# Attention scores from two fp32r parts in the two row halves of the array, with two heads in one exponential

## The chip, the cores and the metric

The kernel runs on one core of one Trainium2 chip. Its time is the device time of the whole kernel in microseconds; three runs of the kernel before took 4031.95, 4031.96 and 4034.76 us, so the median is 4031.96 us. A profile is one further execution, recorded instruction by instruction.

The engines are named as the profile names them: PE multiplies matrices (PEld is its loading of the stationary operand, the "weights"), DVE, ACT and POOL are the vector, activation and general engines, and SP issues most DMAs. PE writes only to PSUM, which has eight banks; one bank holds 512 fp32 numbers in each of 128 partitions.

## The reference

Two layers run one after the other, each an attention block and then an MLP, on an input of 2048 rows by 512 columns in fp32. Each block adds its result to its input.

```python
B, S, D, H = 1, 2048, 512, 32          # so a head has Dh = 16 columns
# attention, on the layer-normed x
qkv = (x @ wqkv).reshape(B, S, 3, H, Dh)
scores = einsum("bhqd,bhkd->bhqk", q, k) * (Dh ** -0.5)
p = softmax(scores)                     # over k
o = einsum("bhqk,bhkd->bhqd", p, v)     # then @ wo
# MLP, F = 1792, on the layer-normed x
h = x @ w1 + b1
act = h * tanh(softplus(h));  return act @ w2
```

The softmax takes the maximum over the 2048 keys from each score, so the kernel needs every score twice in effect: once for the maximum and once for the exponential.

## The kernel before, in words

**Precision.** The dense products (`mm3`, lines 111 to 116) split each fp32 operand into a high and a low fp32r part and add three products. The scores are made otherwise: q and k are split into three bf16 parts each (lines 380 to 389) and the parts are stacked along the contraction. `K_PARTS` and `Q_PARTS` name the six pairs of parts; six pairs of 16 columns give `KROWS` = 96 contraction rows. Two more rows carry the negative maximum of each query (as two bf16 parts, against rows of ones), so that the score matmul of 98 rows (`MROWS`) gives the score less its maximum.

**Groups and steps.** The 32 heads are done in 8 groups of 4 (`HG`). A group has 4 blocks of 512 queries and 16 key tiles of 128 keys, so 64 steps; a layer has 512 steps and the kernel 1024. `prep_qk` (line 186) loads the stacked q and k of a group from a DRAM scratch, half a group ahead; `prep_v` (line 208) lays out the values.

**One step** (`run`, lines 327 to 350) does three things:

- `score` (line 273), once for each of the 4 heads: a matmul of 128 keys by 512 queries into one PSUM bank (line 280, tile `sc`), then the exponential on ACT from this bank into the tile `p` (line 287). The banks come from `pbank("s", ...)`, a pool of three separate one-bank tiles.
- `max_mm` (line 219), four times, for a step 20 steps (`AHEAD`) later: 128 queries by 512 keys (line 236, tile `pm`), two of them into a two-bank tile `mx`, of which there are two; DVE then reduces the 1024 columns to one maximum per query (line 245). After 16 steps `max_fold` and `max_rows` bring the maxima into rows of q by a transpose on PE, two DVE instructions and eight small DMAs.
- `pv` (line 289) for the step before: exponentials times values, four heads in four column groups of the array, in plain fp32 (line 299). The program has 4 such matmuls per step and the profile shows 8, two for each. After 16 steps `out_rows` transposes and divides by the sum.

**The order on PE** is written out by hand. `pe` (line 175) chains every attention matmul to the one before, so PE does them in the order of the calls: score 0, score 1, max 0, 1, 2, score 2, max 3, score 3, `pv` of the step before. What `tick` brings in (`max_rows`, `out_rows`) stands before `pv`. ACT and DVE serve their queues in order too; outside the attention a scheduler orders the instructions.

**Other users of the three "s" banks.** The accumulators `qk` of the q and k projection (line 378, read by an ACT copy and a DVE subtraction), `va` of the values (line 401, read by an ACT copy), the hidden layer `h` of the MLP (line 448, read by an ACT instruction at line 468), and some transposes (`nmt`, `otp`, `op`).

Of the kernel before, what the change touches and what calls it, by code (L numbers as in the profile page):

```python
# [9 lines left out]
F32 = mybir.dt.float32  # L10
F32R = mybir.dt.float32r
BF16 = mybir.dt.bfloat16
AF = mybir.ActivationFunctionType
ALU = mybir.AluOpType
# [4 lines left out]
P = 128  # L19
# [10 lines left out]
SCALE = DH ** -0.5  # L30
HCLAMP = 10.0
LN_HALF = -0.6931471805599453
KROWS = 96
MROWS = 98
K_PARTS = (0, 0, 0, 1, 1, 2)
Q_PARTS = (0, 1, 2, 0, 1, 0)
AHEAD = 20
GSTEPS = NCH * NKT
STEPS = NG * GSTEPS
# [7 lines left out]
def kernel(ctx: ExitStack, tc: tile.TileContext, x, wqkv, wo, w1, b1, w2, out):  # L47
# [14 lines left out]
    nc.gpsimd.memset(mhalf, -0.5)  # L62
    lnhalf = const.tile([P, 1], F32, name="lnhalf")
    nc.gpsimd.memset(lnhalf, LN_HALF)
    ones = const.tile([MROWS - KROWS, 256], BF16, name="ones")
    nc.gpsimd.memset(ones, 1.0)
    b1t = const.tile([P, FT], F32, name="b1t")
    nc.sync.dma_start(b1t, b1.rearrange("(f p) -> p f", p=P))
# [1 line left out]
    def b8(shape, dt, name):  # L70
        return blk.tile(shape, dt, tag="blk", name=name)

    def pbank(tag, name):
        return ps.tile([P, 512], F32, tag=tag, name=name, bufs=3 if tag == "s" else 1)

    def t512(tag, name, dt=F32):
        return tmp.tile([P, 512], dt, tag=tag, name=name, bufs=T_BUFS.get(tag, 2))
# [29 lines left out]
    def split_psum(hi, lo, src):  # L107
        nc.scalar.activation(hi, src, AF.Copy)
        nc.vector.tensor_tensor(lo, src, hi.bitcast(F32), op=ALU.subtract)
# [52 lines left out]
    class Attention:  # L162
# [24 lines left out]
        def prep_qk(self, g):  # L187
            l = self.l
            ks, qs = [], []
            for u in range(HG // 2):  # L190
                k = b8([P, 2, S], BF16, f"ks{l}{g}{u}")
                q = b8([P, 2, S], BF16, f"qs{l}{g}{u}")
                nc.sync.dma_start(
                    k[KROWS:MROWS].rearrange("p h (r n) -> p (h r) n", n=256),
                    ones[:, None, :].to_broadcast([MROWS - KROWS, 2 * S // 256, 256]),
                )
                m, h0 = divmod(g * HG + 2 * u, P // DH)
                for t, parts, base in ((k, K_PARTS, NCH), (q, Q_PARTS, 0)):
                    for j, a in enumerate(parts):
                        nc.sync.dma_start(  # L200
                            t[j * DH : (j + 1) * DH],
                            self.scr[base + m][a, h0 * DH : (h0 + 2) * DH, :].rearrange("(h d) n -> d h n", d=DH),
                        )
                ks.append(k)
                qs.append(q)
            self.qk[g] = (ks, qs)
# [9 lines left out]
                )  # L216
            self.va[g] = va

        def max_mm(self, s, n):
            if s >= STEPS:  # L220
                return
            b, i = divmod(s, NKT)
            g, qb = divmod(b, NCH)
            h, qt = divmod(i, NCH)
            half, j = divmod(n, 2)
            l = self.l
            if n == 0 and s % GSTEPS == GSTEPS // 2 and g + 1 < NG:
                self.prep_qk(g + 1)
            ks, qs = self.qk[g]
            if i == 0 and n == 0:  # L230
                self.mxs[b] = tmp.tile([P, HG, NCH, 2], F32, tag="mxv", name=f"mxv{l}{b}")
            if j == 0:
                self.pm = ps.tile([P, 2, 512], F32, tag="mx", name=f"pm{l}{b}{i}{half}")
            q0 = qb * CW + qt * P
            self.pe(
                nc.tensor.matmul(  # L236
                    self.pm[:, j],
                    qs[h // 2][0:KROWS, h % 2, q0 : q0 + P],
                    ks[h // 2][0:KROWS, h % 2, ts(n, 512)],
                    start=True,  # L240
                    stop=True,
                )
            )
            if j == 1:
                nc.vector.tensor_reduce(self.mxs[b][:, h, qt, half : half + 1], self.pm, axis=AX.XY, op=ALU.max)  # L245
                if i == NKT - 1 and half == 1:
                    self.max_fold(b)

        def max_fold(self, b):
            l = self.l  # L250
# [6 lines left out]
        def max_rows(self, b, nm):  # L257
            g, qb = divmod(b, NCH)
            l = self.l
            _, qs = self.qk[g]  # L260
            tp = pbank("s" if self.running else "acc", f"nmt{l}{b}")
            self.pe(nc.tensor.transpose(tp[0 : HG * NCH, 0:P], nm, ident))
            np_ = tmp.tile([HG * NCH, 2, P], BF16, tag="np", name=f"np{l}{b}")
            nc.vector.tensor_copy(np_[:, 0], tp[0 : HG * NCH, 0:P])
            nc.vector.tensor_tensor(np_[:, 1], tp[0 : HG * NCH, 0:P], np_[:, 0], op=ALU.subtract)
            for h in range(HG):
                for a in range(2):
                    nc.sync.dma_start(
                        qs[h // 2][KROWS + a : KROWS + a + 1, h % 2, ts(qb, CW)].rearrange("o (t n) -> o t n", n=P),
                        np_[h * NCH : (h + 1) * NCH, a, :],  # L270
                    )

        def score(self, s, h):
            b, kt = divmod(s, NKT)
            g, qb = divmod(b, NCH)
            ks, qs = self.qk[g]
            if h == 0:
                self.pts[s] = b8([P, HG, CW], F32, f"p{self.l}{s}")
            sp = pbank("s", f"sc{self.l}{s}{h}")
            self.pe(nc.tensor.matmul(  # L280
                sp,
                ks[h // 2][0:MROWS, h % 2, ts(kt, P)],
                qs[h // 2][0:MROWS, h % 2, ts(qb, CW)],
                start=True,
                stop=True,
            ))
            nc.scalar.activation(self.pts[s][:, h, :], sp, AF.Exp, scale=SCALE)  # L287

        def pv(self, s):
            b, kt = divmod(s, NKT)  # L290
# [18 lines left out]
        def out_rows(self, b, ot):  # L309
            g, qb = divmod(b, NCH)  # L310
            l = self.l
            tp = pbank("s", f"otp{l}{b}")
            for t in range(NCH):
                self.pe(nc.tensor.transpose(tp[:, ts(t, P)], ot[:, ts(t, P)], ident))
            tv = tp.rearrange("p (t h d) -> p t h d", t=NCH, h=HG)
            rc = tmp.tile([P, NCH, HG, 1], F32, tag="rc", name=f"rc{l}{b}")
            nc.vector.reciprocal(rc, tv[:, :, :, DH : DH + 1])
            nc.vector.tensor_tensor(
                self.ost[qb][:, :, ts(g, HG * DH)].rearrange("p t (h d) -> p t h d", d=DH),
                tv[:, :, :, 0:DH],  # L320
                rc.to_broadcast([P, NCH, HG, DH]),
                op=ALU.mult,
            )

        def run(self, hooks, ost, fill):
            ost.extend(b8([P, NCH, D], F32, f"o{self.l}{c}") for c in range(NCH))
            self.ost = ost
            self.prep_v(0)
            self.running = True
            for s in range(STEPS):  # L330
                if s % GSTEPS == GSTEPS - NKT and s // GSTEPS + 1 < NG:
                    self.prep_v(s // GSTEPS + 1)
                self.score(s, 0)
                self.score(s, 1)
                for n in range(3):
                    self.max_mm(s + AHEAD, n)
                self.score(s, 2)
                self.max_mm(s + AHEAD, 3)
                if s + AHEAD >= STEPS:
                    next(fill, None)  # L340
                self.score(s, 3)
                self.tick()
                if s:
                    self.pv(s - 1)
                if s in hooks:
                    hooks[s]()
            self.pv(STEPS - 1)
            self.tick(99)
# [6 lines left out]
                wts[j] = load_rows(wqkv[:, 2 * D : 3 * D], j - 4, f"wv{l}{j}", **kw)  # L355

    def qkv(l, wts, tt, order, late):
        scr = [dram.tile([3, P, S], BF16, name=f"scr{l}{m}") for m in range(2 * NCH)]
        att = Attention(l, scr)
        ahead = [0]  # L360

        def some_max():
            if ahead[0] < AHEAD:
                att.chained = True
                att.tick()
                for n in range(4):
                    att.max_mm(ahead[0], n)
                ahead[0] += 1

        done = 0  # L370
        for m, c in order:
            if c not in tt:
                late()
            w = wts[m // 2]
            pt = tmp.tile([P, 3, CW], BF16, tag="raw", name=f"pt{l}{m}{c}", bufs=3)
            th, tl = tt[c]
            acc = pbank("s", f"qk{l}{c}{m}")
            mm3(
# [1 line left out]
                [(w[:, 0, k, ts(m % 2, P)], w[:, 1, k, ts(m % 2, P)], th[:, k], tl[:, k]) for k in range(KT)],  # L380
                pe=att.pe,
            )
            p0, p1, p2 = (pt[:, a] for a in range(3))
            r = t512("f", f"pr{l}{c}{m}")
            nc.scalar.activation(p0, acc, AF.Copy)
            nc.vector.tensor_tensor(r, acc, p0, op=ALU.subtract)  # L386
            nc.scalar.activation(p1, r, AF.Copy)
            nc.gpsimd.tensor_tensor(p2, r, p1, op=ALU.subtract)
            nc.scalar.dma_start(scr[m][:, :, ts(c, CW)].rearrange("a p n -> p a n"), pt)
            if (m, c) == (5, 3) and 4 not in wts:  # L390
                load_qkv(l, wts, (4, 5), behind=True)
            if m in (0, 4):
# [235 lines left out]
```

## Time and profile before

| what | value |
|---|---|
| median of three runs | 4031.96 us |
| span of the profiled execution | 4036.3 us (0.1% above the median; no other time of this execution is recorded) |
| PE busy | 3985.8 us, 99% of the span |
| DVE, ACT, POOL busy | 76%, 67%, 14% |
| first and last score matmul of the kernel | 195.4 us, 3668.9 us |
| granted PE clock, mean | 0.996 of full speed |

An instruction's time in the profile runs from its start to its modelled end. Matmuls overlap, so the distance from one start to the next is what a matmul costs PE in a stream, and its own duration is what a reader of its result waits for. In a grouped row ("x3") the duration is the union over the group. `<-` names what an engine waited for.

### The profile page before, as it was taken

Reading aid. Unit: us, or ns where it says so; the run is one execution under the profiler, and the core shown is the slowest. Engines: PE = TensorE matmul, PEld = TensorE weight load, DVE = VectorE, ACT = ScalarE, POOL = GpSimd, SP = SyncE. Lnnn points to the kernel's source line nnn. Section 1 sums busy time; section 2 is a strip of 40 time slices with the busy share of each in tenths; the row PEclk is TensorE's granted clock in tenths of the full one; section 3 lists DMA queues with packets and bytes.
Section 4 is the critical chain, followed back from the end, with each engine's and each line's share of the span. In section 5 each row is a group of like instructions: output and inputs, shape, how many; then the busy total and the mean of one; then the engine's idle time right before and its main releaser. Section 6 shows DMA issues by size and latency. Waiting matters only on the chain.

```text
span 4036.3 us, 54209 instructions
## 1 busy us (share of the span) xinstructions
PE 3985.8 (99%) x21312; PEld 1753.5 (43%) x21312; DVE 3075.2 (76%) x3266; ACT 2697.6 (67%) x4875; POOL 568.7 (14%) x465
## 2 busy tenths in 40 slices
PE   7999999999999999999999999999999999999999
PEld 5733333333333333687766333333333333336887
DVE  5588888888888888566555888888888888875655
ACT  3377777777777777544443777777777777775444
POOL 3200000000000020354431000000000000203545
PEclk9999999999999999999999999999999999999999
DMA  5220120202020200100042110201010201011000
GB/s 167 79 32 11 23 33 1 33 1 33 1 33 1 32 22 32 58 11 11 22 138 78 21 22 12 33 1 32 1 33 1 32 8 26 22 32 58 11 11 22
DMA packets 79535, 124.10 MB, mean 31 GB/s; under 512 B 14256, under 2 KB 51120, under 8 KB 79280
## 3 DMA queue, kind: packets, MB, share of 16 engines
q1 hardware_dynamic: 48848, 88.12, 10.9%
q10 hardware_dynamic: 30432, 32.51, 2.4%
q8 instruction: 168, 2.75, 0.3%
q14 instruction: 87, 0.71, 0.1%
HBM read 85.99 MB, written 33.55 MB: 30 GB/s over the span
## 4 chain that ended last, share of the span: by engine, by line
PE 48%; DVE 3%; POOL 1%; ACT 1%; issue 0%; DMA 0%; POOLq 0%; DVEq 0%; SPq 0%; ACTq 0%
PE pv L299 13%; PE sc L280 12%; PE pm L236 11%; PE mo L116 1%; PE h L114 1%; PE h L116 1%; PE h L115 1%; PE mo L114 1%; PE mo L115 1%; POOL hb L477 1%; DVE al L478 1%; PE qk L114 1%; PE qk L115 1%; POOL hb L474 1%; PE qk L116 1%
## 5 line engine op out<-in xcount | busy, mean ns | idle before, releaser
L245 DVE TENSOR_REDUCE mxv<-pm 128x1 f32<-128x1024 f32 x2048 | 2414.3, 1220 | 512.4 <-PE pm L236 506.5
L287 ACT ACTIVATE p<-sc 128x512 f32<-128x512 f32 x4096 | 2208.1, 596 | 667.3 <-PE sc L280 667.3
L280 PE MATMUL sc<-qs,ks 98*128 98x512 bf16 x4096 | 1390.9, 382 | 0.2
L236 PE MATMUL pm<-ks,qs 96*128 96x512 bf16 x4096 | 1214.4, 379 | 2.7 <-DMA ks<-scr 1.4
L299 PE MATMUL pv<-p,va 128*32 128x512 f32 x8192 | 1090.5, 605 | 0.0
L280 PEld LDWEIGHTS <-ks 98*128 98x128 bf16 x4096 | 314.7, 97 | 1108.4 <-issue 866.4
L236 PEld LDWEIGHTS <-qs 96*128 96x128 bf16 x4096 | 396.4, 98 | 491.5 <-issue 12.9
L210 POOL MEMSET va<- 128x2048 f32 x16 | 28.9, 1806 | 2419.9 <-PE pv L299 2233.4
L299 PEld LDWEIGHTS pv<-p,va 128*32 128x32 f32 x8192 | 161.4, 108 | 406.0 <-issue 385.2
L474 POOL TENSOR_TENSOR hb<-hb,he 128x512 f32<-128x512 f32 x112 | 157.7, 1408 | 186.2 <-DVE he L471 179.3
L477 POOL TENSOR_TENSOR hb<-hb,hr 128x512 f32<-128x512 f32 x112 | 160.9, 1437 | 135.8 <-DVE ah L476 114.5
L114 PE MATMUL mo<-w,ah 128*128 128x512 f32 x448 | 178.9, 399 | 0.7 <-DVE ah L476 0.7
L114 PE MATMUL h<-thm,w 128*128 128x512 f32 x448 | 176.6, 394 | 1.6 <-ACT hb L468 1.6
L115 PE MATMUL mo<-w,ah 128*128 128x512 f32 x448 | 177.1, 395 | 0.0
L472 ACT ACTIVATE hr<-he 128x512 f32<-128x512 f32 x112 | 70.9, 633 | 157.9 <-DVE he L471 79.2
L116 PE MATMUL h<-thm,w 128*128 128x512 f32 x448 | 175.9, 393 | 0.0
L115 PE MATMUL h<-tlm,w 128*128 128x512 f32 x448 | 175.8, 392 | 0.0
L478 DVE TENSOR_TENSOR al<-hb,ah 128x512 fp32r<-128x512 f32 x112 | 111.8, 998 | 83.8 <-POOL hb L477 83.8
L116 PE MATMUL mo<-w,al 128*128 128x512 f32 x448 | 163.2, 401 | 7.5 <-DVE al L478 7.5
L470 ACT ACTIVATE he<-he 128x512 f32<-128x512 f32 x112 | 70.8, 632 | 102.0 <-DVE he L469 99.0
L476 DVE TENSOR_TENSOR ah<-hb,hr 128x512 fp32r<-128x512 f32 x112 | 76.9, 686 | 62.5 <-ACT hr L473 42.9
L114 PE MATMUL qk<-thq,wqk 128*128 128x512 f32 x256 | 110.6, 434 | 7.9 <-DVE pr L386 4.4
(167 smaller groups left out, 2637.8 us busy)
## 6 DMA issues: line engine op xcount, KB each, us to landing
scr<-pt ACTq DMA_DIRECT2D x64, 384.0 KB
qs<-scr SPq DMA_DIRECT2D x192, 128.0 KB
ks<-scr SPq DMA_DIRECT2D x192, 128.0 KB
qs<-np SPq DMA_DIRECT2D x512, 1.0 KB
x<-in_A_x_dram SPq DMA_DIRECT2D x7, 1024.0 KB
xs<-x SPq DMA_DIRECT2D x4, 1024.0 KB
x<-xs SPq DMA_DIRECT2D x4, 1024.0 KB
out_dram<-x SPq DMA_DIRECT2D x3, 1024.0 KB
```

Of the source, the lines that this page charges most:

```text
L114: pe(nc.tensor.matmul(acc, ah, bh, start=first and i == 0, stop=False))
L115: pe(nc.tensor.matmul(acc, ah, bl, start=False, stop=False))
L116: pe(nc.tensor.matmul(acc, al, bh, start=False, stop=last and i == n - 1))
L236: nc.tensor.matmul(self.pm[:, j], qs[h // 2][0:KROWS, h % 2, q0 : q0 + P], ks[h // 2][0:KROWS, h % 2, ts(n, 512)], start=True, stop=True,)
L245: nc.vector.tensor_reduce(self.mxs[b][:, h, qt, half : half + 1], self.pm, axis=AX.XY, op=ALU.max)
L280: self.pe(nc.tensor.matmul(sp, ks[h // 2][0:MROWS, h % 2, ts(kt, P)], qs[h // 2][0:MROWS, h % 2, ts(qb, CW)], start=True, stop=True,))
L287: nc.scalar.activation(self.pts[s][:, h, :], sp, AF.Exp, scale=SCALE)
L299: self.pe(nc.tensor.matmul(acc[ts(h, VW), :], va[:, kt, h, :], pt[:, h, :], start=kt == 0, stop=kt == NKT - 1))
L474: nc.gpsimd.tensor_tensor(hb, hb, e, op=ALU.mult)
L476: nc.vector.tensor_tensor(ah, hb, r, op=ALU.mult)
L477: nc.gpsimd.tensor_tensor(hb, hb, r, op=ALU.mult)
L478: nc.vector.tensor_tensor(al, hb, ah.bitcast(F32), op=ALU.subtract)
```

## The change

The scores and the maxima are made from two fp32r parts instead of three bf16 parts. Three pairs of parts give 48 contraction rows, 50 with the maxima. An even head of the group lies in partitions 0 to 49, an odd head in partitions 64 to 113, so that the matmuls of two heads use different row halves of the array. fp32r matmuls have no separate weight-load instruction in the program; PE loads the weights as a part of them.

The three "s" banks become one tile `s3` of three banks, allocated once; `pbank("s", ...)` hands out its thirds in turn. In a step, the score matmuls come in three units, `UNITS`: heads 0 and 1 into two neighbouring banks with one exponential of 1024 columns, then head 2, then head 3, with one exponential of 512 columns each. The banks of the units are 0 and 1, 2, 0 in an even step and 1 and 2, 0, 1 in an odd step.

`max_mm` is called twice per step instead of four times; each call makes the maxima matmuls of two heads over 512 keys and one DVE reduction of 1024 columns to two maxima. The transposes `nmt` and `otp` move from the "s" banks to the `mx` tiles. The projection's split into three parts (ACT, DVE, ACT, POOL) becomes `split_psum`, a split into two (an ACT copy and a DVE subtraction); the scratch takes 512 KB instead of 384 KB per write, and `prep_qk` issues 28 DMAs per group instead of 26. The order on PE becomes unit 0, max, unit 1, max, unit 2, `pv` of the step before.

```diff
-KROWS = 96
-MROWS = 98
-K_PARTS = (0, 0, 0, 1, 1, 2)
-Q_PARTS = (0, 1, 2, 0, 1, 0)
+KROWS = 48
+MROWS = 50
+HALF = 64
+K_PARTS = (0, 0, 1)
+Q_PARTS = (0, 1, 0)
+UNITS = (((0, 2, 0), (2, 1, 2), (3, 1, 0)), ((0, 2, 1), (2, 1, 0), (3, 1, 2)))
...
+    s3 = ps.tile([P, 3, 512], F32, tag="s", name="s3", bufs=1)
+    turn = [0]
+
     def pbank(tag, name):
-        return ps.tile([P, 512], F32, tag=tag, name=name, bufs=3 if tag == "s" else 1)
+        if tag == "s":
+            turn[0] = (turn[0] + 1) % 3
+            return s3[:, turn[0]]
+        return ps.tile([P, 512], F32, tag=tag, name=name, bufs=1)
...
         def prep_qk(self, g):
-                k = b8([P, 2, S], BF16, f"ks{l}{g}{u}")
-                q = b8([P, 2, S], BF16, f"qs{l}{g}{u}")
+                k = b8([P, S], F32R, f"ks{l}{g}{u}")
+                q = b8([P, S], F32R, f"qs{l}{g}{u}")
...
+                for e in range(2):
+                    r0 = e * HALF
...
+                    for t, parts, base in ((k, K_PARTS, NCH), (q, Q_PARTS, 0)):
+                        for j, a in enumerate(parts):
+                            nc.sync.dma_start(
+                                t[r0 + j * DH : r0 + (j + 1) * DH].bitcast(F32),
+                                self.scr[base + m][a, (h0 + e) * DH : (h0 + e + 1) * DH, :].bitcast(F32),
+                            )
...
-        def max_mm(self, s, n):
+        def max_mm(self, s, half):
...
+            pm = ps.tile([P, 2, 512], F32, tag="mx", name=f"pm{l}{b}{u}{i}")
+            for e in range(2):
+                rows = slice(e * HALF, e * HALF + KROWS)
+                self.pe(
+                    nc.tensor.matmul(
+                        pm[:, e], qs[u][rows, q0 : q0 + P], ks[u][rows, ts(n, 512)], start=True, stop=True
+                    )
                 )
+            nc.vector.tensor_reduce(self.mxs[b][:, 2 * u : 2 * u + 2, qt, n], pm, axis=AX.X, op=ALU.max)
...
-            tp = pbank("s" if self.running else "acc", f"nmt{l}{b}")
+            tp = ps.tile([P, 2, 512], F32, tag="mx", name=f"nmt{l}{b}")[:, 0]
...
-        def score(self, s, h):
+        def score(self, s, unit):
+            h0, n, bank = UNITS[s % 2][unit]
...
+            for h in range(h0, h0 + n):
+                rows = slice(h % 2 * HALF, h % 2 * HALF + MROWS)
+                self.pe(
+                    nc.tensor.matmul(
+                        s3[:, bank + h - h0],
+                        ks[h // 2][rows, ts(kt, P)],
+                        qs[h // 2][rows, ts(qb, CW)],
+                        start=True,
+                        stop=True,
+                    )
+                )
+            nc.scalar.activation(self.pts[s][:, h0 : h0 + n], s3[:, bank : bank + n], AF.Exp, scale=SCALE)
...
         def run(self, hooks, ost, fill):
                 self.score(s, 0)
+                self.max_mm(s + AHEAD, 0)
                 self.score(s, 1)
-                for n in range(3):
-                    self.max_mm(s + AHEAD, n)
-                self.score(s, 2)
-                self.max_mm(s + AHEAD, 3)
+                self.max_mm(s + AHEAD, 1)
                 if s + AHEAD >= STEPS:
                     next(fill, None)
-                self.score(s, 3)
+                self.score(s, 2)
                 self.tick()
                 if s:
                     self.pv(s - 1)
...
-            p0, p1, p2 = (pt[:, a] for a in range(3))
-            r = t512("f", f"pr{l}{c}{m}")
-            nc.scalar.activation(p0, acc, AF.Copy)
-            nc.vector.tensor_tensor(r, acc, p0, op=ALU.subtract)
-            nc.scalar.activation(p1, r, AF.Copy)
-            nc.gpsimd.tensor_tensor(p2, r, p1, op=ALU.subtract)
-            nc.scalar.dma_start(scr[m][:, :, ts(c, CW)].rearrange("a p n -> p a n"), pt)
+            split_psum(pt[:, 0], pt[:, 1], acc)
+            nc.scalar.dma_start(
+                scr[m][:, :, ts(c, CW)].bitcast(F32).rearrange("a p n -> p a n"), pt.bitcast(F32)
+            )
```

More of the change, by code (lines that the diff above doesn't have):

```diff
@@ L64 @@
     nc.gpsimd.memset(lnhalf, LN_HALF)
-    ones = const.tile([MROWS - KROWS, 256], BF16, name="ones")
+    ones = const.tile([MROWS - KROWS, 256], F32, name="ones")
     nc.gpsimd.memset(ones, 1.0)
@@ L190, in prep_qk @@
             for u in range(HG // 2):
-                k = b8([P, 2, S], BF16, f"ks{l}{g}{u}")
-                q = b8([P, 2, S], BF16, f"qs{l}{g}{u}")
[L193 to L196, printed above, removed]
-                m, h0 = divmod(g * HG + 2 * u, P // DH)
[L198 to L203, printed above, removed]
+                k = b8([P, S], F32R, f"ks{l}{g}{u}")
+                q = b8([P, S], F32R, f"qs{l}{g}{u}")
+                m, h0 = divmod(g * HG + 2 * u, P // DH)
+                for e in range(2):
+                    r0 = e * HALF
+                    nc.sync.dma_start(
+                        k[r0 + KROWS : r0 + MROWS].bitcast(F32).rearrange("p (r n) -> p r n", n=256),
+                        ones[:, None, :].to_broadcast([MROWS - KROWS, S // 256, 256]),
+                    )
+                    for t, parts, base in ((k, K_PARTS, NCH), (q, Q_PARTS, 0)):
+                        for j, a in enumerate(parts):
+                            nc.sync.dma_start(
+                                t[r0 + j * DH : r0 + (j + 1) * DH].bitcast(F32),
+                                self.scr[base + m][a, (h0 + e) * DH : (h0 + e + 1) * DH, :].bitcast(F32),
+                            )
                 ks.append(k)
@@ L223, in max_mm @@
             g, qb = divmod(b, NCH)
-            h, qt = divmod(i, NCH)
-            half, j = divmod(n, 2)
+            u, i = divmod(2 * i + half, GSTEPS // 4)
+            qt, n = divmod(i, NCH)
             l = self.l
-            if n == 0 and s % GSTEPS == GSTEPS // 2 and g + 1 < NG:
+            if half == 0 and s % GSTEPS == GSTEPS // 2 and g + 1 < NG:
                 self.prep_qk(g + 1)
             ks, qs = self.qk[g]
[L230 to L233, printed above, removed]
+            if u == 0 and i == 0:
+                self.mxs[b] = tmp.tile([P, HG, NCH, NCH], F32, tag="mxv", name=f"mxv{l}{b}")
+            pm = ps.tile([P, 2, 512], F32, tag="mx", name=f"pm{l}{b}{u}{i}")
             q0 = qb * CW + qt * P
[L235 to L241, printed above, removed]
-                )
[L243 to L247, printed above, removed]
+            for e in range(2):
[4 more added lines that the diff above has]
+                    )
+                )
+            nc.vector.tensor_reduce(self.mxs[b][:, 2 * u : 2 * u + 2, qt, n], pm, axis=AX.X, op=ALU.max)
+            if u == 1 and i == GSTEPS // 4 - 1:
+                self.max_fold(b)
         def max_fold(self, b):
@@ L260, in max_rows @@
             _, qs = self.qk[g]
-            tp = pbank("s" if self.running else "acc", f"nmt{l}{b}")
+            tp = ps.tile([P, 2, 512], F32, tag="mx", name=f"nmt{l}{b}")[:, 0]
             self.pe(nc.tensor.transpose(tp[0 : HG * NCH, 0:P], nm, ident))
-            np_ = tmp.tile([HG * NCH, 2, P], BF16, tag="np", name=f"np{l}{b}")
+            np_ = tmp.tile([HG * NCH, 2, P], F32R, tag="np", name=f"np{l}{b}", bufs=1)
             nc.vector.tensor_copy(np_[:, 0], tp[0 : HG * NCH, 0:P])
-            nc.vector.tensor_tensor(np_[:, 1], tp[0 : HG * NCH, 0:P], np_[:, 0], op=ALU.subtract)
+            nc.vector.tensor_tensor(np_[:, 1], tp[0 : HG * NCH, 0:P], np_[:, 0].bitcast(F32), op=ALU.subtract)
             for h in range(HG):
                 for a in range(2):
+                    r = (h % 2) * HALF + KROWS + a
                     nc.sync.dma_start(
-                        qs[h // 2][KROWS + a : KROWS + a + 1, h % 2, ts(qb, CW)].rearrange("o (t n) -> o t n", n=P),
-                        np_[h * NCH : (h + 1) * NCH, a, :],
+                        qs[h // 2][r : r + 1, ts(qb, CW)].bitcast(F32).rearrange("o (t n) -> o t n", n=P),
+                        np_[h * NCH : (h + 1) * NCH, a, :].bitcast(F32),
                     )
-        def score(self, s, h):
+        def score(self, s, unit):
             b, kt = divmod(s, NKT)
@@ L276, in score @@
             ks, qs = self.qk[g]
-            if h == 0:
+            h0, n, bank = UNITS[s % 2][unit]
+            if h0 == 0:
                 self.pts[s] = b8([P, HG, CW], F32, f"p{self.l}{s}")
[L279 to L287, printed above, removed]
+            for h in range(h0, h0 + n):
[10 more added lines that the diff above has]
+            nc.scalar.activation(self.pts[s][:, h0 : h0 + n], s3[:, bank : bank + n], AF.Exp, scale=SCALE)
         def pv(self, s):
@@ L311, in out_rows @@
             l = self.l
-            tp = pbank("s", f"otp{l}{b}")
+            tp = ps.tile([P, 2, 512], F32, tag="mx", name=f"otp{l}{b}")[:, 0]
             for t in range(NCH):
@@ L357, in qkv @@
     def qkv(l, wts, tt, order, late):
-        scr = [dram.tile([3, P, S], BF16, name=f"scr{l}{m}") for m in range(2 * NCH)]
+        scr = [dram.tile([2, P, S], F32R, name=f"scr{l}{m}") for m in range(2 * NCH)]
         att = Attention(l, scr)
@@ L365, in some_max @@
                 att.tick()
-                for n in range(4):
+                for n in range(2):
                     att.max_mm(ahead[0], n)
@@ L374, in qkv @@
             w = wts[m // 2]
-            pt = tmp.tile([P, 3, CW], BF16, tag="raw", name=f"pt{l}{m}{c}", bufs=3)
+            pt = tmp.tile([P, 2, CW], F32R, tag="raw", name=f"pt{l}{m}{c}", bufs=3)
             th, tl = tt[c]
@@ L382, in qkv @@
             )
-            p0, p1, p2 = (pt[:, a] for a in range(3))
-            r = t512("f", f"pr{l}{c}{m}")
-            nc.scalar.activation(p0, acc, AF.Copy)
-            nc.vector.tensor_tensor(r, acc, p0, op=ALU.subtract)
-            nc.scalar.activation(p1, r, AF.Copy)
-            nc.gpsimd.tensor_tensor(p2, r, p1, op=ALU.subtract)
-            nc.scalar.dma_start(scr[m][:, :, ts(c, CW)].rearrange("a p n -> p a n"), pt)
+            split_psum(pt[:, 0], pt[:, 1], acc)
+            nc.scalar.dma_start(
+                scr[m][:, :, ts(c, CW)].bitcast(F32).rearrange("a p n -> p a n"), pt.bitcast(F32)
+            )
             if (m, c) == (5, 3) and 4 not in wts:
```

## The prediction

> **What bounds the kernel now.** I read the page first (busy times), then the cores (clock), then the groups by line, then the timeline inside the attention. The page and the groups:
>
> ```profile
> span 4036.3 us, 54209 instructions
> PE 3985.8 (99%) x21312; PEld 1753.5 (43%) x21312; DVE 3075.2 (76%) x3266; ACT 2697.6 (67%) x4875; POOL 568.7 (14%) x465
> ...
> L245 DVE TENSOR_REDUCE mxv<-pm 128x1 f32<-128x1024 f32 x2048 | 2414.3, 1220 | 512.4 <-PE pm L236 506.5
> L287 ACT ACTIVATE p<-sc 128x512 f32<-128x512 f32 x4096 | 2208.1, 596 | 667.3 <-PE sc L280 667.3
> L280 PE MATMUL sc<-qs,ks 98*128 98x512 bf16 x4096 | 1390.9, 382 | 0.2
> ...
> L299 PE MATMUL pv<-p,va 128*32 128x512 f32 x8192 | 1090.5, 605 | 0.0
> ...
> L470 ACT ACTIVATE he<-he 128x512 f32<-128x512 f32 x112 | 70.8, 632 | 102.0 <-DVE he L469 99.0
> ```
>
> PE is busy throughout, and its score matmuls sat idle for 0.2 us in all: it never waits. ACT waits for PE (667.3 us) and DVE waits for PE (506.5 us). 4096 scores at four per step are 1024 steps. One step in the timeline of the attention (start, duration, instruction):
>
> ```profile
> 1003.26 0.38 PE L280 MATMUL sc<-qs,ks 98*128 98x512 bf16 x1
> ...
> 1003.57 1.06 PE L299 MATMUL pv<-p,va 128*32 128x512 f32 x8
> ...
> 1004.57 0.60 PE L280 MATMUL sc<-qs,ks 98*128 98x512 bf16 x2
> ...
> 1004.99 2.17 ACT L287 ACTIVATE p<-sc 128x512 f32<-128x512 f32 x4 [0.67 <-PE sc L280]
> 1005.01 0.81 PE L236 MATMUL pm<-ks,qs 96*128 96x512 bf16 x3
> ...
> 1005.64 2.36 DVE L245 TENSOR_REDUCE mxv<-pm 128x1 f32<-128x1024 f32 x2 [0.48 <-PE pm L236]
> 1005.66 0.38 PE L280 MATMUL sc<-qs,ks 98*128 98x512 bf16 x1
> ...
> 1005.88 0.38 PE L236 MATMUL pm<-ks,qs 96*128 96x512 bf16 x1
> ...
> 1006.10 0.38 PE L280 MATMUL sc<-qs,ks 98*128 98x512 bf16 x1
> ...
> 1006.41 1.06 PE L299 MATMUL pv<-p,va 128*32 128x512 f32 x8
> ```
>
> From `pv` to `pv` a step is 1006.41 - 1003.57 = 2.84 us: `pv` 1.00 (1003.57 to 1004.57), seven matmul pitches of 0.22 (1004.57 to 1006.10), and 0.31 from the last score to `pv`. What makes this possible is that three scores can be ahead of ACT: PE passes each bank wait without stopping.
>
> **The change, part by part.** *Where the score matmuls wait.* This decides the sum. Before, a score writes one of three tiles, so it waits for the exponential three scores back. After, the three banks are one tile `s3`, and in the built program every unit waits for the exponential just before it, whatever its bank: unit 1 for the 1024-column exponential of unit 0 of its own step, unit 2 for that of unit 1, unit 0 for that of unit 2 of the step before. So units and exponentials alternate strictly, and `pv`, chained behind unit 2, stands in the same chain. The step becomes a sum of latencies. Their prices are in this stretch, where PE waits for ACT before a fp32r matmul:
>
> ```profile
> 1978.89 0.60 PE L149 MATMUL tpq<-ident,xnq 128*128 128x128 f32 x4
> ...
> 1979.53 0.60 ACT L108 ACTIVATE thq<-tpq 128x512 fp32r<-128x512 f32 x1 [2.52 <-PE tpq L149]
> ...
> 1980.02 0.68 ACT L468 ACTIVATE hb<-h,b1t 128x512 f32<-128x512 f32 x1
> ...
> 1980.16 0.69 DVE L109 TENSOR_TENSOR tlq<-tpq,thq 128x512 fp32r<-128x512 f32 x1 [2.36 <-ACT thq L108]
> 1980.76 0.19 PEld L114 LDWEIGHTS h<-thm,w 128*128 128x128 f32 x1 [0.76 <-ACT hb L468]
> 1980.76 0.50 PE L114 MATMUL h<-thm,w 128*128 128x512 f32 x1 [0.33 <-ACT hb L468]
> ...
> 1980.86 0.19 PEld L115 LDWEIGHTS h<-tlm,w 128*128 128x128 f32 x1
> 1981.10 0.40 PE L115 MATMUL h<-tlm,w 128*128 128x512 f32 x1
> ...
> 1981.34 0.40 PE L116 MATMUL h<-thm,w 128*128 128x512 f32 x1
> ```
>
> PE to ACT takes 1979.53 - 1979.49 = 0.04; ACT to PE 1980.76 - 1980.70 = 0.06. A matmul that had to wait lasts 0.50, where its followers last 0.40: its weights load after the wait and cost 0.10. The next weights follow 0.10 later (1980.86). In a stream fp32r costs 0.24 per matmul.
>
> - Unit 0: 0.10 for the first head's weights, 0.10 for the second's, 0.40: 0.60. If both ran from the same moment 0.50; if the halves don't overlap 0.34 + 0.40 = 0.74. I take 0.60, since the rows show the weights 0.10 apart, and eight `pv` matmuls of 0.6 each in 1.00 show that parts of the array do run together.
> - Its exponential: 0.596 for 512 columns; another 512 cost 0.425, by this row of 1024 against the 0.632 of L470 above: 1.02.
>
> ```profile
> L89 ACT ACTIVATE wqk<-wqk00r x1: 1057/1057/1057, 8.4 to 8.4; 128x1024 fp32r<-128x1024 f32 x1
> ```
>
> - Unit 1: 0.50; its exponential 0.60. Each way between engines 0.04 and 0.06.
> - Unit 2 to `pv`: 0.31 as now, and 0.10 of weights; `pv` 1.00. The exponential of unit 2 (0.50 + 0.04 + 0.60 + 0.06 = 1.20) ends inside these 1.41.
>
> Step: 0.60 + 0.04 + 1.02 + 0.06 + 0.50 + 0.04 + 0.60 + 0.06 + 0.41 + 1.00 = 4.33 us, between 4.23 and 4.47 by the bounds of unit 0. Against 2.84 that is +1.49 in 1024 steps: +1526 us (+1423 to +1669).
>
> *What is gained and hidden.* The maxima matmuls in fp32r, in two halves or not, lie behind units 0 and 1: four matmuls in a row are at most 0.34 + 3 x 0.24 = 1.06, and PE waits until 1.72 after unit 0. If they were slower by 0.6 the cover would be gone. ACT work falls from 2.17 to 1.02 + 2 x 0.60 less overlap; DVE keeps its two reductions of 1024 (2.36). Neither is late in 4.33, so both gains are worth nothing. The `mx` tiles come free in time: the first reduction ends some 2.4 after unit 0, the second 3.7, both before their tile is next written; so `nmt` and `otp`, now in `mx` tiles, find one free and cost PE what they cost before. Loads of q and k (28 DMAs a group on SP's queue for 26, the same bytes) have 32 steps to land, the eight row DMAs per block 18: hidden, and at worst a few us per layer at the first group.
>
> *Projection.* Here too an accumulator now waits until the one before is read: 0.16 (end of the last matmul beyond its pitch) + 0.04 + 1.32 (1979.53 to 1980.85, the same ACT copy and DVE subtraction) + 0.06 + 0.10 = 1.68. Half of the 64 have a maximum step behind them, whose 0.88 (4 x 0.22, on PE's path before) hides in it. 32 x 1.68 + 32 x 0.80 = 80; for 24 of the 32 value accumulators 0.16 + 0.04 + 0.60 + 0.06 + 0.10 = 0.96 each, 23; less some 8 at the start, where PE waits for data anyway: +95. Bounds 0 (the scheduler finds other work) and 64 x 1.68 + 32 x 0.96 = 138. The POOL subtraction that goes was hidden except before the first group; I count nothing.
>
> *MLP.* Twelve `mo` matmuls (2.8 us) stand between two `h` accumulators and cover the 0.9 of an ACT read. Nothing; with ACT late, at most 112 x 0.33 (the wait of the row above) = 37.
>
> Sum: 4036.3 + 1526 + 95 = 5658 on the profile's span, which is 0.1% above the median; on the median 4032 + 1621 = 5653, so 5650. With all bounds of this case 5455 to 5876. The row halves matter little: without overlap 5650 + 0.14 x 1024 = 5793. By the Trainium skill (TensorEngine Tiling (Array Packing), Overview) two row tiles give up to twice the speed, so 5650 rather than 5793; the rows have only column groups running together.
>
> **The rivals.** *The PE clock falls.* Now PE never pauses in the attention and the clock is 1.00. After, it stands still twice per step, some 0.8 us after unit 0's matmuls and 0.5 after unit 1's. Two places show what pauses do (PE busy second, PEclk behind POOL):
>
> ```profile
> 1970.00:1971.00 1.00, 0.33 (x2) 0.00 (x0) 0.26 (x1) 1.00 (x2) 0.00 (x0) 1.00 0.00 0
> 1971.00:1972.00 1.00, 0.00 (x0) 0.00 (x0) 1.00 (x2) 0.78 (x2) 0.00 (x0) 1.00 0.00 0
> 1972.00:1973.00 1.00, 0.37 (x2) 0.33 (x3) 0.96 (x2) 0.00 (x0) 0.00 (x0) 1.00 0.00 0
> 1973.00:1974.00 1.00, 1.00 (x6) 0.82 (x5) 1.00 (x3) 0.00 (x0) 0.00 (x0) 1.00 0.00 0
> 1974.00:1975.00 1.00, 1.00 (x5) 0.74 (x3) 0.24 (x2) 0.63 (x1) 0.00 (x0) 0.54 0.00 0
> ...
> 2040.00:2045.00 5.00, 2.81 (x14) 1.93 (x12) 3.63 (x6) 2.60 (x5) 1.15 (x2) 1.00 0.12 46
> ```
>
> ```profile
> 1975.42 0.63 PE L115 MATMUL h<-tlm,w 128*128 128x512 f32 x1
> ```
>
> With 1.70 busy of 4 us the clock halved; with 2.81 of 5 (56%) it stayed. After the change the page's measure of PE busy would be some 3 of 4.33, so on average above, but a stretch without `pv` is nearer the place that fell. Price: at half clock a matmul lasts 0.63 instead of 0.40, weights twice 0.10, `pv` 0.85 more, the way from unit 2 to it 0.31 more: a step of 1.03 + 0.04 + 1.02 + 0.06 + 0.83 + 0.04 + 0.60 + 0.06 + 0.72 + 1.85 = 6.25. In half of the steps that gives 5650 + 512 x 1.92 = 6630, in all 7620. By the Trainium skill (TensorE: Matmul & The Clock Gate, "A second HAM failure mode: psum-queue depth-cycling") a PE that idles briefly between groups while it cycles through banks lets its clock oscillate; the table under "Why this matters for your kernels" asks only for no gaps above about 3 us, and by that the clock would stay and the time be 5650. The rows above disagree with the second: the gap there was 2.3 us.
>
> *The waits act per bank.* Then unit 2 alone waits for unit 0's exponential: 0.60 + 0.04 + 1.02 + 0.06 + 0.41 + 1.00 = 3.13, and 4032 + 0.29 x 1024 + 95 = 4424. The rotation of banks speaks for it, the program's waits against it.
>
> *Faster.* If no wait for ACT stood in PE's chain, PE would need `pv` 1.00 + 0.31 and five pitches of 0.24 (the pairs side by side), 2.51, and DVE its 2.36 of reductions: 4032 - 0.33 x 1024 + 95 = 3789. It decides where the chain of waits falls below 2.84. Only a program in which unit 2 can start before unit 0's exponential ends would do it.
>
> **How the numbers follow.** Strict alternation at about full clock: 0.53, 5650, its own range 5455 to 5876. The same with a clock that falls: 0.37, of it 0.22 up to half of the steps and 0.15 beyond. Per bank: 0.06. Faster: 0.03, no change within 0.2% (about what a measurement tells here): 0.01. So slower 0.96. The range takes the first case and the second up to somewhat over half of the steps: 5430 to 6900, leaving out 0.07 below and some 0.13 above.
>
> **What would show it.** In the groups, ACT's exponentials wait for PE three times per step and PE's scores wait for ACT by some 1.3 us per step; `pv` to `pv` 4.3; DVE busy near 2.4 of it; PE's share near 70%. In the projection PE waits 1 to 1.7 us per accumulator for DVE. PEclk of 0.9 or more says first case, below that the clock. The prediction is wrong if unit 1 starts before unit 0's exponential ends, or if the step is under 4.2 at full clock.

## The result and the profile after

The changed kernel takes 7567.22 us (median of four runs, 7565.51 to 7571.12) against 4031.95 us before in the same comparison. The ratio is 1.877, with a 95% interval of 1.874 to 1.879. The forecast was slower, 5650 us, with a range of 5430 to 6900: the direction and the place were right, the time lies above the range. It lies 0.7% below the 7620 us that the prediction worked out for its first rival, a clock that is halved in all steps.

The page of the changed kernel (busy times, the PE clock in 40 slices in tenths, the chain that ended last, groups with busy time, mean ns and the idle time before them):

```profile
span 7565.1 us, 53935 instructions
...
PE 6333.5 (84%) x21312; PEld 2427.3 (32%) x21312; DVE 3161.8 (42%) x3266; ACT 2728.4 (36%) x3787; POOL 480.9 (6%) x401
...
PEclk8755555555555555559986555555555555555599
...
PE 69%; ACT 23%; issue 3%; DVE 3%; POOL 1%; DMA 1%; ACTq 0%; SPq 0%; POOLq 0%; DVEq 0%
...
L251 DVE TENSOR_REDUCE mxv<-pm 128x2 f32<-128x1024 f32 x2048 | 2509.5, 1226 | 3647.7 <-PE pm L247 3647.7
L298 ACT ACTIVATE p<-s 128x512 f32<-128x512 f32 (+1 forms) x3072 | 2270.2, 739 | 3873.3 <-PE s L290 3057.0
L290 PE MATMUL s<-qs,ks 50*128 50x512 f32 x4096 | 2411.3, 785 | 1059.1 <-ACT p L298 1057.7
...
L310 PE MATMUL pv<-p,va 128*32 128x512 f32 x8192 | 1971.4, 1056 | 0.0
```

ACT is 23% of the chain. Before, it was 1%:

```profile
PE 48%; DVE 3%; POOL 1%; ACT 1%; issue 0%; DMA 0%; POOLq 0%; DVEq 0%; SPq 0%; ACTq 0%
```

PE's scores now wait for ACT (1057.7 us) while ACT waits for them (3057.0): two engines that take turns. The values matmuls, which the change doesn't touch, went from 1090.5 to 1971.4 us busy, as the clock fell: PEclk shows fives through both attention stages and nines in the MLP between them.

One step in the timeline (start, duration, instruction):

```profile
1002.11 0.79 PE L290 MATMUL s<-qs,ks 50*128 50x512 f32 x2
...
1002.71 0.63 PE L247 MATMUL pm<-ks,qs 48*128 48x512 f32 x2
1003.01 1.02 ACT L298 ACTIVATE p<-s 128x1024 f32<-128x1024 f32 x1 [2.06 <-PE s L290]
...
1004.09 0.79 PE L290 MATMUL s<-qs,ks 50*128 50x512 f32 x1 [0.75 <-ACT p L298]
...
1004.09 1.21 PE L247 MATMUL pm<-ks,qs 48*128 48x512 f32 x2
1004.92 0.60 ACT L298 ACTIVATE p<-s 128x512 f32<-128x512 f32 x1 [0.88 <-PE pm L247]
...
1005.57 0.79 PE L290 MATMUL s<-qs,ks 50*128 50x512 f32 x1 [0.26 <-ACT p L298]
...
1006.29 1.93 PE L310 MATMUL pv<-p,va 128*32 128x512 f32 x8
1006.39 0.60 ACT L298 ACTIVATE p<-s 128x512 f32<-128x512 f32 x1 [0.88 <-PE s L290]
...
1008.15 0.79 PE L290 MATMUL s<-qs,ks 50*128 50x512 f32 x2
```

Read it as a staircase: unit 0, its exponential, unit 1, its exponential, unit 2, `pv`, and the next unit 0 at 1008.15. A step is 6.04 us. No score starts before the exponential ahead of it has ended. The two matmuls of unit 0 together last 0.79, as long as one of unit 1: the halves do run side by side.

Where the clock went is seen at the first steps of the attention. The scores of the timeline, and three windows (PE busy is the first pair after the commas, the PE clock stands behind POOL):

```profile
279.30 0.57 PE L290 MATMUL s<-qs,ks 50*128 50x512 f32 x2 [0.69 <-ACT v L417]
...
280.98 0.50 PE L290 MATMUL s<-qs,ks 50*128 50x512 f32 x1 [0.89 <-ACT p L298]
...
282.17 0.50 PE L290 MATMUL s<-qs,ks 50*128 50x512 f32 x1 [0.45 <-ACT p L298]
283.35 0.80 PE L290 MATMUL s<-qs,ks 50*128 50x512 f32 x2 [0.69 <-ACT p L298]
```

```profile
279.00:283.00 4.00, 2.03 (x8) 0.84 (x8) 2.45 (x2) 2.16 (x4) 0.40 (x1) 1.00 0.01 4
283.00:287.00 4.00, 2.70 (x8) 1.26 (x8) 1.70 (x2) 1.92 (x3) 0.00 (x0) 0.54 0.00 0
287.00:291.00 4.00, 3.55 (x13) 0.72 (x13) 1.16 (x2) 1.43 (x2) 0.00 (x0) 0.50 0.01 1
```

The first step runs at full clock and its latencies are those of the prediction: 1.68 from unit 0 to unit 1 (1.72 forecast), 1.19 from unit 1 to unit 2 (1.20). PE is busy for half of these 4 us; then the clock is at half, and over the whole attention its mean is 0.51.

### The profile page after: what moved, and what is told of

Its sections match the earlier page's. It is cut to its first block, busy times and chain, and to the rows that moved or that the text cites. A ratio compares the mean times of both kernels' runs of the same rounds, so it can differ in the third digit from the quotient of the medians.

```text
span 7565.1 us, 53935 instructions
## 1 busy us (share of the span) xinstructions
PE 6333.5 (84%) x21312; PEld 2427.3 (32%) x21312; DVE 3161.8 (42%) x3266; ACT 2728.4 (36%) x3787; POOL 480.9 (6%) x401
## 3 DMA queue, kind: packets, MB, share of 16 engines
q8 instruction: 168, 2.75, 0.1%
## 4 chain that ended last, share of the span: by engine, by line
PE 69%; ACT 23%; issue 3%; DVE 3%; POOL 1%; DMA 1%; ACTq 0%; SPq 0%; POOLq 0%; DVEq 0%
PE s L290 31%; PE pv L310 25%; ACT p L298 22%; PE s L122 3%; PE s L124 2%; PE s L123 2%; PE mo L124 1%; PE mo L122 1%; PE mo L123 1%; PE otp L325 1%; PE wo L122 1%; DVE pt L117 1%; PE wo L124 0%; DVE al L484 0%; PE pm L247 0%
## 5 line engine op out<-in xcount | busy, mean ns | idle before, releaser
L251 DVE TENSOR_REDUCE mxv<-pm 128x2 f32<-128x1024 f32 x2048 | 2509.5, 1226 | 3647.7 <-PE pm L247 3647.7
L298 ACT ACTIVATE p<-s 128x512 f32<-128x512 f32 (+1 forms) x3072 | 2270.2, 739 | 3873.3 <-PE s L290 3057.0
L290 PE MATMUL s<-qs,ks 50*128 50x512 f32 x4096 | 2411.3, 785 | 1059.1 <-ACT p L298 1057.7
L290 PEld LDWEIGHTS s<-qs,ks 50*128 50x128 f32 x4096 | 869.9, 282 | 4194.9 <-ACT p L298 2508.4
L310 PE MATMUL pv<-p,va 128*32 128x512 f32 x8192 | 1971.4, 1056 | 0.0
L247 PE MATMUL pm<-ks,qs 48*128 48x512 f32 x4096 | 1814.8, 652 | 14.3 <-DMA ks<-scr 13.8
L247 PEld LDWEIGHTS pm<-ks,qs 48*128 48x128 f32 x4096 | 812.6, 312 | 31.7 <-issue 30.6
L122 PE MATMUL s<-thq,wqk 128*128 128x512 f32 x256 | 127.0, 496 | 88.8 <-DVE pt L117 88.1
L122 PE MATMUL s<-thm,w 128*128 128x512 f32 x448 | 178.3, 398 | 8.8 <-ACT hb L474 8.6
L124 PE MATMUL s<-thm,w 128*128 128x512 f32 x448 | 176.3, 394 | 0.0
L123 PE MATMUL s<-tlm,w 128*128 128x512 f32 x448 | 174.7, 390 | 0.0
L124 PE MATMUL s<-thq,wqk 128*128 128x512 f32 x256 | 119.0, 465 | 0.0
```

Source lines behind the costliest of these rows:

```text
L122: pe(nc.tensor.matmul(acc, ah, bh, start=first and i == 0, stop=False))
L123: pe(nc.tensor.matmul(acc, ah, bl, start=False, stop=False))
L124: pe(nc.tensor.matmul(acc, al, bh, start=False, stop=last and i == n - 1))
L247: nc.tensor.matmul(pm[:, e], qs[u][rows, q0 : q0 + P], ks[u][rows, ts(n, 512)], start=True, stop=True)
L251: nc.vector.tensor_reduce(self.mxs[b][:, 2 * u : 2 * u + 2, qt, n], pm, axis=AX.X, op=ALU.max)
L290: nc.tensor.matmul(s3[:, bank + h - h0], ks[h // 2][rows, ts(kt, P)], qs[h // 2][rows, ts(qb, CW)], start=True, stop=True,)
```

## The experiments

Theory A is the prediction's: the three banks in one tile make every unit wait for the exponential before it; to it comes now that this idleness halves the clock. The rivals lay the clock or the loss on the fp32r matmuls in row halves (B), on the amount of such work (C), or say that the two-head exponential is a gain as soon as the waits are mended (D). Each experiment whose time stands without a ratio was executed once.

**Own banks.** The one tile is undone, and with it the exponential of two heads; the rest of the change stays:

```diff
-    s3 = ps.tile([P, 3, 512], F32, tag="s", name="s3", bufs=1)
...
+        return ps.tile([P, 512], F32, tag=tag, name=name, bufs=3 if tag == "s" else 1)
...
-            nc.scalar.activation(self.pts[s][:, h0 : h0 + n], s3[:, bank : bank + n], AF.Exp, scale=SCALE)
+            for h in range(h0, h0 + n):
+                nc.scalar.activation(self.pts[s][:, h], banks[h - h0], AF.Exp, scale=SCALE)
```

> The changed kernel with one part undone: the three score banks are three separate tiles again, each head has its own exponential of 512 columns, and everything else (fp32r parts, row halves, order of the maxima, split) stays. Theory A (the one tile makes every score unit wait for the exponential just before it, PE stands still and its clock halves): the only wait left in a step is head 3 for the exponential of head 0, 0.10 + 0.40 + 0.04 + 0.60 + 0.06 = 1.20 after head 0, then 0.41 to the values matmuls and 1.00 for them, so 2.6 us per step, granted clock 0.95 or more, about 3800 us (3700 to 4000). Rival B (fp32r matmuls in row halves are themselves what lowers the clock or PE's speed): clock well under 0.9 and more than 4500 us.

Measured: 3930.32 us, ratio 0.976 to the kernel before (0.974 to 0.977), clock 0.993. Its timeline:

```profile
1001.58 0.50 PE L285 MATMUL sc<-qs,ks 50*128 50x512 f32 x2
...
1002.76 0.50 PE L285 MATMUL sc<-qs,ks 50*128 50x512 f32 x1
...
1003.19 1.07 PE L306 MATMUL pv<-p,va 128*32 128x512 f32 x8
...
1004.19 0.50 PE L285 MATMUL sc<-qs,ks 50*128 50x512 f32 x2
```

This step is 2.61 us (2.6 expected), and its head 3 starts 1.18 after head 0. The time is 130 us above the 3800 expected: from the first to the last score of an attention (1410 and 1407 us) a step takes 2.75 us in the mean, so not all steps go like this one. PE's waits of the two kinds of transposes for DVE make 22.8 us each of it, its waits of scores for the maxima rows 14.0; the rest stays open. The scores start at 195.5 us as before, so the loss in the projection goes with the tile too. B falls: with the fp32r halves kept, the kernel is faster than before. That the tile alone does the harm, and not the two-head exponential, is for the next run to show.

**The one tile alone**, in the kernel before, with bf16 parts, full rows and four exponentials:

```diff
+    s3 = ps.tile([P, 3, 512], F32, tag="s", name="s3", bufs=1)
...
-        return ps.tile([P, 512], F32, tag=tag, name=name, bufs=3 if tag == "s" else 1)
+        if tag == "s":
+            turn[0] = (turn[0] + 1) % 3
+            return s3[:, turn[0]]
...
```

> The kernel before with one part of the change alone: its three score banks become one tile of three banks; bf16 parts, full rows, one exponential per head and the old order stay. Theory A: every score waits for the exponential just before it, 3 x (0.38 + 0.04 + 0.60 + 0.06) + 0.31 + 1.00 = 4.55 us per step at full clock, 5900 us; and PE stands still some 1.7 us of it, so the clock may fall here too: at half clock 3 x 1.33 + 0.52 + 1.85 = 6.36 us per step, 7700 us. Rival B (the clock falls because of fp32r and row halves): clock 0.95 or more, so at most 5900 us.

Measured 7853.06 us:

```profile
core 0: 7851.3 us, clock 0.637
```

```profile
PE s L286 <- ACT p L293: 1029.4, 2041, 1.0
```

The scores, which sat idle for 0.2 us in the kernel before, now wait 1029.4 us for the exponentials. So the one tile by itself makes a loss as large, and the clock falls without fp32r and without row halves. This settles A against B.

**More work on PE.** In the changed kernel each pair of maxima matmuls is done twice, and three times; the repeats write the same numbers to the same place.

```diff
-            for e in range(2):
+            for e in (0, 1) * 3:
```

> The changed kernel, with each pair of maxima matmuls done twice into the same place (the second overwrites the first with the same numbers): 4096 more matmuls on PE and nothing else. Theory A with the clock set by how long PE stands still: the extra matmuls fall into PE's waits, PE stands still some 0.4 us less per step; if this is enough the clock comes back and the step is 4.3 us, 5700 us, in spite of more work; if not, 6.0 to 6.1 us per step and about 7600 us. Rival C (the clock falls with the amount of fp32r work in row halves, by its power or its form): not faster than 7567 us, clock at or below 0.58.

> The same with each pair of maxima matmuls done three times: 8192 more matmuls. Theory A: PE stands still some 0.8 us less per step than in the changed kernel; the clock is 0.9 or more and the time about 5700 us. If the clock stayed at half, the repeated matmuls would no longer fit behind the exponentials (0.86 more behind unit 1) and the step would be about 6.6 us, 8100 us. Rival C: 8100 us or more.

Measured: 6909.52 us with two, between the two times that were expected, and 5780.77 us with three. Clock, and a step of the second:

```profile
core 0: 6907.7 us, clock 0.704
```

```profile
core 0: 5779.0 us, clock 0.974
```

```profile
1001.02 0.50 PE L290 MATMUL s<-qs,ks 50*128 50x512 f32 x2
...
1001.36 0.86 PE L247 MATMUL pm<-ks,qs 48*128 48x512 f32 x6
1001.62 1.02 ACT L298 ACTIVATE p<-s 128x1024 f32<-128x1024 f32 x1 [1.11 <-PE s L290]
...
1002.70 0.49 PE L290 MATMUL s<-qs,ks 50*128 50x512 f32 x1 [0.48 <-ACT p L298]
...
1003.88 0.50 PE L290 MATMUL s<-qs,ks 50*128 50x512 f32 x1
...
1005.31 0.50 PE L290 MATMUL s<-qs,ks 50*128 50x512 f32 x2
```

8192 useless matmuls make the kernel 1786 us faster. At full clock the alternation is there unchanged, and the step is 4 hundredths from the forecast: 1005.31 - 1001.02 = 4.29 against 4.33. C falls. The loss of 3535 us splits in two: some 1750 from the alternation (5781 - 4032), the waits outside the attention among them, and at least 1786 from the clock.

**What the clock goes by.** Does PE's standing still count, or how much of the array works? The maxima matmul of the even head three times and of the odd head once adds as many matmuls as doing the pair twice, but one behind the other, so they fill as much time as the pair three times:

```diff
-            for e in range(2):
+            for e in (0, 1, 0, 0):
```

> The changed kernel, with the maxima matmul of the even head (lower row half) done three times and that of the odd head once: two more matmuls per pair, as in the run with each pair done twice, but one after the other, so they fill as much of PE's waiting time as in the run with each pair done three times (0.48 us per pair at full clock). If the clock goes by how long PE stands still: as with three pairs, clock 0.95 or more and about 5780 us. If it goes by how much of the array works: as with two pairs, clock about 0.70 and 6900 us.

Measured 7084.55 us:

```profile
core 0: 7082.7 us, clock 0.671
```

```profile
539.81 0.87 PE L247 MATMUL pm<-ks,qs 48*128 48x512 f32 x4
541.15 0.50 PE L290 MATMUL s<-qs,ks 50*128 50x512 f32 x1 [0.47 <-ACT p L298]
```

```profile
284.00:296.00 12.00, 12.00 (x44) 5.62 (x48) 4.94 (x5) 4.47 (x7) 0.00 (x0) 0.50 0.12 16
```

It is near the pair done twice (0.704) and far from three times (0.974). Yet the time is filled as intended: at full clock the four matmuls behind unit 0 take 0.87 us and unit 1 waits 0.47, against 0.86 and 0.48 with three pairs. At half clock PE does not stand still at all, 12.00 of 12 us in the window, and the clock stays at 0.50. So filling PE's time is not enough; what counted here is nearer to the amount of work in the array. The number of matmuls would fit as well, since this run has as many as the one with two pairs.

**Two tiles**, so that heads 0 and 1 share an exponential without all units waiting in a row:

```diff
-    s3 = ps.tile([P, 3, 512], F32, tag="s", name="s3", bufs=1)
+    s2 = ps.tile([P, 2, 512], F32, tag="s", name="s2", bufs=1)
+    s1 = ps.tile([P, 1, 512], F32, tag="s1", name="s1", bufs=1)
...
-            h0, n, bank = UNITS[s % 2][unit]
+            h0, n, bank = UNITS[0][unit]
+            st, bank = (s1, 0) if bank == 2 else (s2, bank)
...
```

> The changed kernel with its three score banks as two tiles, one of two banks and one of one bank: heads 0 and 1 use the first, head 2 the second, head 3 the first bank of the first, in every step; the exponential of two heads stays. Theory A: head 3 waits only for the exponential of heads 0 and 1, so the step is 1.68 (unit 0 to the end of its exponential, as the first full-clock step of the changed kernel shows) + 0.43 + 1.00 = 3.1 us with one pause of PE of some 0.6 us; by the clock of the runs so far (0.97 with pauses of 0.5 us, 0.70 with longer ones) it stays above 0.9, and the time is about 4310 us, slower than before. If the clock falls all the same the step is 4.6 us, 5800 us. Rival D (the exponential of two heads is a gain as soon as waits are per tile): not over 4032 us.

Measured 4343.8 us:

```profile
core 0: 4342.0 us, clock 0.994
```

```profile
1001.02 0.50 PE L292 MATMUL s<-qs,ks 50*128 50x512 f32 x2
...
1002.70 0.50 PE L292 MATMUL s<-qs,ks 50*128 50x512 f32 x1 [0.47 <-ACT p L300]
...
1004.12 0.50 PE L292 MATMUL s<-qs,ks 50*128 50x512 f32 x2
```

3.10 us per step, as expected, and slower than before by 310 us although the clock is full. With three banks, an exponential over two of them keeps head 3, which needs a bank of the pair, waiting until 1.68 us after unit 0; D falls for three banks.

**One row half.** The first experiment with all scores and maxima matmuls in the lower half (two of the four heads' scores are left out and the others stand in for them):

```diff
-                rows = slice(e * HALF, e * HALF + KROWS)
+                rows = slice(0, KROWS)
...
-                rows = slice(h % 2 * HALF, h % 2 * HALF + MROWS)
+                rows = slice(0, MROWS)
```

> The first experiment with every score and maxima matmul reading the lower row half (rows 0 to 49), so no two can run side by side; heads 1 and 3 are then computed from the q and k of heads 0 and 2, which leaves their own scores out. Loads, instructions and order are the same. If the row halves run side by side in the first experiment: 0.10 + 7 x 0.24 + 0.31 + 1.00 = 3.1 us per step instead of 2.6, 4420 us, slower than before. If they never overlapped: the time of the first experiment, 3930 us.

Measured 4620.47 us:

```profile
core 0: 4618.6 us, clock 0.937
```

```profile
1000.07 1.06 PE L306 MATMUL pv<-p,va 128*32 128x512 f32 x8
...
1003.14 1.07 PE L306 MATMUL pv<-p,va 128*32 128x512 f32 x8
```

3.07 us per step at full clock (3.1 expected) against 2.61 with both halves: the halves are worth 0.46 us per step. The time is 200 us above the 4420 expected, and the clock dips here too.

**The transposes back.** The first experiment with `nmt` and `otp` in the score banks, as before the change:

> The first experiment (own banks, an exponential per head), and the transposes nmt and otp back in the score banks as in the kernel before. There PE waited 22.8 us each for DVE before them. If these waits go and nothing comes in their place, 3880 us; if the score banks make PE wait for ACT instead, 3930 us as in the first experiment.

Measured 3919.52 us, ratio 0.971 (0.969 to 0.973), the fastest kernel here. It is 11 us under the first experiment; the two were measured in different comparisons and their intervals just miss each other, so the gain is small at best. Where PE waits in the attention now:

```profile
PE sc L285 <- DMA qs<-np: 21.7, 19, 2.9
PE sc L285 <- ACT p L294: 10.2, 23, 0.5
```

The two waits of 22.8 us for DVE are gone; that for the maxima rows rose from 14.0 to 21.7, and 10.2 for ACT is new.

## Why the prediction was right and wrong

**Right: the place of the loss.** Strict alternation of units and exponentials, with `pv` in the chain. Each price at full clock held: 1.68 for 1.72, 1.19 for 1.20, 4.29 for 4.33 per step in the run with three pairs; the weights' 0.10 after a wait shows in the matmuls of 0.50; and the waits of 0.89 and 0.45 in the first step are the 1.3 per step that were forecast. One term was a little dear: from unit 0 to its exponential 0.60 us pass (1001.02 to 1001.62 above), where 0.64 was summed.

**Right: what was counted at nothing.** DVE is at 42%, ACT at 36%; the maxima, the transposes in `mx` tiles and the loads end no wait of size (the largest is 13.8 us in all, for loads of k).

**Wrong: the chance and the range.** The step that failed is the weighing of the first rival: "After the change the page's measure of PE busy would be some 3 of 4.33, so on average above", which gave the full clock 0.53, the halved one beyond half of the steps 0.15, and a range that ended at 6900. The price of that rival was right: 6.25 us per step worked out, 6.04 measured (most of it unit 0 again: 0.90 from its start to ACT, 1002.11 to 1003.01, where 1.07 had been summed), 7620 us worked out and 7567 measured. What was wrong was to compare the clock with the share of time in which PE is busy, and to take the row with 56% for a share that holds it. After its first fall the clock came back 29 times within the two attention stages, by the trace's record of the clock, each time for one stretch of 3.41 us. The first such stretch:

```profile
392.52:395.93 3.41, 2.02 (x12) 0.78 (x8) 2.04 (x2) 1.62 (x2) 0.00 (x0) 1.00 0.00 0
```

PE is busy for 59% of it, and the clock falls at its end all the same. The stretch holds units 0 to 2 and hardly any `pv`; the prediction had a doubt about such stretches, but went by the average. And the run with the lower half done three times shows that filled time alone does not hold the clock. I also took a fallen clock for something that comes back and stays. PE is busy 84% of the span by the page, and the clock was at 0.50 for nearly all of both attention stages.

One small sum is off as well: the cases below 5430 have 0.06, 0.03 and 0.01, so the range left out 0.10 below, not 0.07.

**Wrong in size: the projection.** +95 us was summed, from waits. Outside the attention the kernel lost 199: the first score came 84 us later, the stretch between the two attentions took 94 us longer, the stretch after the second 21. The waits were near the sum. From the list of PE's waits (total, times, longest): the scores in the attention, then the accumulators of the projection, of the values and of the MLP:

```profile
PE s L290 <- ACT p L298: 1057.7, 2010, 1.2
PE s L122 <- DVE pt L117: 91.5, 59, 4.3
PE s L122 <- ACT v L417: 15.1, 22, 0.7
...
PE s L122 <- ACT hb L474: 8.6, 21, 0.9
```

They are 1.55 us each for DVE, where 1.68 was forecast for half of them and 0.80 for the others. The rest lies in slower matmuls: those of the projection's third product, which wait for nothing, went from a mean of 404 ns to 465 (line 116 before, then line 124 after).

```profile
L116 PE MATMUL qk<-thq,wqk 128*128 128x512 f32 x256 | 103.3, 404 | 0.0
```

```profile
L124 PE MATMUL s<-thq,wqk 128*128 128x512 f32 x256 | 119.0, 465 | 0.0
```

Here too the clock falls (its mean is 0.79 from 100 to 200 us), and the sum had no term for it.

By the Trainium skill (TensorE: Matmul & The Clock Gate, "A second HAM failure mode: psum-queue depth-cycling") short idle times between matmul groups are enough to let the clock oscillate. The trace agrees that it falls, with the mean at 0.58, though in the attention it mostly stays down. The rule in the same page's "Why this matters for your kernels", no gaps above about 3 us, does not hold here: PE's longest wait for an exponential was 1.2 us.

## What to carry to other kernels

Buffers that are to be free one by one are best allocated one by one: slices of one tile may share their waits, as they did here, and the built program's waits tell before any run. Where a change makes PE take turns with another engine, price the step at both clocks, and lean to the low one when the array works little in the step, however busy PE looks. A bank more per instruction is no gain when banks are what the pipeline runs on.

## What the runs showed of the hardware

- A kernel became 1786 us faster by doing 8192 matmuls more (clock 0.58 to 0.97). Twice the pair gave 0.70, between the two.
- The clock fell with a longest PE wait of 1.2 us, and also in the run with one row half, where PE was busy 98% by the page and the mean clock was 0.937. With one wait of 0.47 us in a 3.1 us step that uses both halves it was 0.994. At a clock of 0.50 even a PE that was busy for all of 12 us did not bring it back. What exactly the clock goes by stays open; the share of busy time isn't it.
- Two fp32r matmuls of 50 rows in the two row halves take the time of one (0.50 for both, 3.07 against 2.61 us per step without and with).
